# Projecting the first half of chunk 0 by blocks of the contraction, with twelve accumulation groups open in six PSUM banks

## The chip, the core and the metric

One core of one Trainium2 chip runs the kernel. The metric is the device time in microseconds (us) of one execution. PE is TensorE, PEld its weight loads, DVE VectorE, ACT ScalarE, POOL GpSimd and SP the engine that issues the DMAs. Times "at 7.13" are us from the start of the profiled span.

## The reference, cut to what matters

```python
x = A_x                                   # 1 x 2048 x 512, bf16
xn = layernorm(x)
s = A_ref(xn, wqkv, wo)                   # q, k, v = xn @ wqkv (512 x 1536); dilated local attention; @ wo
g = silu(B_ref(xn, w_gate, w_up, w_down)) # gelu(xn @ w_gate) * (xn @ w_up) @ w_down
return x + s * g
```

The contraction of `xn @ wqkv` runs over 512 rows, which are four blocks of 128.

## The kernel before

The kernel works on four chunks of 512 rows, each made of four tiles of 128. A tile must be normalized (VectorE), transposed (PE) and copied out of PSUM (ScalarE or VectorE) before PE can multiply it with `wqkv`. Chunk 0 is projected in halves: tiles 0 and 1 first, while tiles 2 and 3 arrive. `wqkv` is read in three column loads, q, then k, then v. While PE waits for data it multiplies constants ("warm-ups"), because its clock starts at half speed.

```python
for t in range(TPQ - 1):
    load_x(t)
load_w(wqkv_sb, A_wqkv, 0, D)                      # the columns of q
load_x(TPQ - 1)
for i in range(1, 3):
    load_w(wqkv_sb, A_wqkv, i * D, (i + 1) * D)    # of k, then of v
# ... cut ...
warm_up(18, TQ // 2)
warm_up(4, P)
first_moments(0)
first_moments(1)
first_normalize(0)
transpose(0)
first_normalize(1)
warm_up(4, P)                      # between the tiles' transposes
transpose(1, parts=2)              # two half copies, both on ScalarE
warm_up(4, P)
first_moments(2)
# ... cut: tile 3's moments, the normalizations of tiles 2 and 3 ...
for dks in ((0, 1), (2, 3)):       # q of the first half: 16 matmuls of 256 columns
    for fo in range(NC):
        project(qs[fo], wqkv_sb, fo * P, 0, 0, HQ, dks)
# ... cut: the copies of q, then k in halves, then v in one piece of 512 columns ...
def qkv(j, fo, i0=0, n=TQ, ps=None):
    # ... cut ...
        vst = sm4.tile([P, TQ], BF16, name="vst")
        nc.scalar.activation(out=vst[:], in_=ps, func=AF.Copy)
        nc.sync.dma_start(out=vT[c * P : (c + 1) * P, lo : lo + TQ], in_=vst[:])  # 4 stores of v per chunk
```

v goes to DRAM in four stores of 128 KB per chunk and comes back rearranged as `v_arr`, in four loads of 520 KB.

The softmax here doesn't subtract the row's maximum and nothing guards it: scores larger than these inputs give would overflow.

## Time and profile before

| | before |
|---|---|
| time, median of the first three runs | 229.21 us (229.19 to 229.28) |
| span of the profiled execution (229.35 us) | 227.65 us |
| clock of PE rises to full | at 6.75 |
| transposes of tile 0, of tile 1 start | 5.19, 6.02 |
| first projection matmul | 7.13 |
| transposes of tile 4 (the first after the projection of chunk 0) | 18.01 |
| last matmul starts | 223.94 |

The rows are starts read from the trace. Between 7.13 and 223.94 PE hardly ever waits, so an event moved at the start moves the end by the same amount, unless another wait takes it back.

In this execution the three columns of `wqkv` landed at 6.44, 8.11 and 10.26.

### The profile page before, as it was taken

How to read it: one execution, taken by the hardware profiler on the slowest of the kernel's cores; microseconds unless marked ns; L12 is line 12 of the kernel's file. 1: busy time of each engine (PE TensorE's matmuls, PEld its weight loads, DVE VectorE, ACT ScalarE, POOL GpSimd, SP SyncE). 2: the span in 40 equal slices, each digit the busy share in tenths (PEclk: the TensorE clock that was granted, in tenths of full speed). 3: DMA queues.
4: the chain of work that ended last, by engine and by line, in shares of the span. 5: the costliest groups of instructions: out<-in, count | busy, mean ns of one | idle time of the engine just before them, and what ended most of it. 6: DMA issues, size and time to landing. Idle time of an engine off the chain costs nothing.

```text
span 227.6 us, 3610 instructions
## 1 busy us (share of the span) xinstructions
PE 223.2 (98%) x1320; PEld 107.4 (47%) x1320; DVE 150.4 (66%) x274; ACT 135.0 (59%) x220; POOL 18.1 (8%) x67
## 2 busy tenths in 40 slices
PE   8999999999999999999999999999999999999993
PEld 6874444444444444444444444444444444444453
DVE  4693980899995578979904759924944358971434
ACT  3779779767532666767751566667753357656210
POOL 1047601000040000230000000000000000000000
PEclk9999999999999999999999999999999999999999
DMA  5999399972039911100219921110207950001001
GB/s 167 371 396 387 88 216 175 226 204 76 19 76 206 217 30 29 23 14 0 93 33 199 208 83 27 22 23 0 92 14 150 197 140 0 0 1 32 0 34 60
DMA packets 31266, 24.64 MB, mean 108 GB/s; under 512 B 10896, under 2 KB 31248, under 8 KB 31248
## 3 DMA queue, kind: packets, MB, share of 16 engines
q1 hardware_dynamic: 31248, 24.41, 44.4%
q8 instruction: 10, 0.16, 0.3%
q14 instruction: 8, 0.07, 0.2%
HBM read 18.74 MB, written 4.34 MB: 101 GB/s over the span
## 4 chain that ended last, share of the span: by engine, by line
PE 97%; ACT 1%; DVE 0%; issue 0%; DVEq 0%
PE y_ps L428 21%; PE u_ps L245 21%; PE g_ps L245 21%; PE qkv_ps L245 17%; PE s_ps L444 6%; PE L_ps L323 3%; PE o_ps L391 3%; PE warm_ps L227 2%; PE q_ps L245 1%; PE tr L210 1%; ACT L416 1%; PE den_ps L343 0%; ACT xnT L219 0%; ACT ge L416 0%; ACT vst L269 0%; DVE m L452 0%
## 5 line engine op out<-in xcount | busy, mean ns | idle before, releaser
L245 PE MATMUL u_ps<-xnT,wu_sb 128*128 128x512 bf16 x224 | 57.5, 379 | 0.0
L245 PE MATMUL g_ps<-xnT,wg_sb 128*128 128x512 bf16 x224 | 57.5, 379 | 0.0
L428 PE MATMUL y_ps<-wd_sb,h 128*128 128x512 bf16 (+1 forms) x238 | 49.9, 367 | 0.0
L420 DVE TENSOR_TENSOR h<-ge,u 128x512 bf16<-128x512 bf16 x56 | 23.8, 425 | 32.4 <-ACT u L418 30.9
L416 ACT ACTIVATE ge<-g_ps 128x512 bf16<-128x512 f32 x56 | 33.5, 598 | 16.4 <-PE g_ps L245 16.2
L418 ACT ACTIVATE u<-u_ps 128x512 bf16<-128x512 f32 x56 | 33.5, 598 | 16.1 <-PE u_ps L245 16.1
L305 DVE TENSOR_TENSOR pk<-q_sb,k_sb 128x1024 bf16<-128x1024 bf16 (+1 forms) x56 | 39.0, 761 | 4.6 <-ACT k_sb L266 4.6
L245 PE MATMUL qkv_ps<-xnT,wqkv_sb 128*128 128x512 bf16 (+1 forms) x208 | 40.6, 355 | 0.0
L377 DVE TENSOR_TENSOR pv<-E,v_arr 128x1024 bf16<-128x1024 bf16 (+1 forms) x48 | 39.7, 862 | 0.0
L428 PEld LDWEIGHTS <-h 128*128 128x128 bf16 x238 | 23.0, 98 | 25.9 <-issue 1.3
L245 PEld LDWEIGHTS <-wu_sb 128*128 128x128 bf16 x224 | 21.9, 98 | 26.7 <-issue 0.3
L245 PEld LDWEIGHTS <-wg_sb 128*128 128x128 bf16 x224 | 21.6, 98 | 26.4 <-issue 0.8
L245 PEld LDWEIGHTS <-wqkv_sb 128*128 128x128 bf16 x224 | 21.7, 98 | 19.7 <-DMA xnT<-xn 0.3
L436 ACT ACTIVATE sl<-y_ps 128x512 bf16<-128x512 f32 (+1 forms) x17 | 9.7, 572 | 32.6 <-PE y_ps L428 32.6
L452 DVE TENSOR_TENSOR m<-s_ps,sl 128x512 bf16<-128x512 f32 (+1 forms) x17 | 11.1, 655 | 18.4 <-PE s_ps L444 18.4
L403 DVE TENSOR_TENSOR oT<-o_ps,rb 128x1024 bf16<-128x1024 f32 x8 | 9.4, 1219 | 12.3 <-DMA rb<-rs_d 12.3
L444 PE MATMUL s_ps<-wo_sb,oT 128*128 128x512 bf16 (+1 forms) x68 | 14.8, 367 | 0.0
L195 POOL TENSOR_TENSOR rstd<-rstd,mhalf 128x1 f32<-128x1 f32 x12 | 7.9, 662 | 68.7 <-DVE rstd L192 68.7
L266 ACT ACTIVATE k_sb<-qkv_ps 128x512 bf16<-128x512 f32 (+1 forms) x20 | 10.2, 516 | 3.5 <-PE qkv_ps L245 3.2
L269 ACT ACTIVATE vst<-qkv_ps 128x512 bf16<-128x512 f32 x16 | 9.6, 597 | 4.5 <-PE qkv_ps L245 4.5
L263 ACT ACTIVATE q_sb<-qkv_ps 128x512 bf16<-128x512 f32 (+1 forms) x16 | 8.7, 544 | 3.2 <-PE qkv_ps L245 3.0
L444 PEld LDWEIGHTS <-oT 128*128 128x128 bf16 x68 | 6.6, 98 | 7.2
(49 smaller groups left out, 116.1 us busy)
## 6 DMA issues: line engine op xcount, KB each, us to landing
v_arr<-vT SPq DMA_DIRECT2D x16, 520.0 KB, 8.7
vT<-vst SPq DMA_DIRECT2D x16, 128.0 KB, 1.7
out_dram<-o_t SPq DMA_DIRECT2D x15, 128.0 KB, 3.2
wg_sb<-in_B_w_gate_dram SPq DMA_DIRECT2D x2, 896.0 KB, 9.8
wu_sb<-in_B_w_up_dram SPq DMA_DIRECT2D x2, 896.0 KB, 11.0
wd_sb<-in_B_w_down_dram SPq DMA_DIRECT2D x1, 1792.0 KB, 12.4
wqkv_sb<-in_A_wqkv_dram SPq DMA_DIRECT2D x3, 512.0 KB, 4.9
x_sb<-in_A_x_dram SPq DMA_DIRECT2D x3, 512.0 KB, 10.7
```

Of the source, the lines that this page charges most:

```text
L245: nc.tensor.matmul(ps, lhsT=w[:, dk, lo : lo + P], rhs=xnT[j][:, dk, i0 : i0 + n], start=(dk == 0), stop=(dk == NC - 1),)
L266: nc.scalar.activation(out=k_sb[j][:, c, lo : lo + n], in_=ps, func=AF.Copy)
L269: nc.scalar.activation(out=vst[:], in_=ps, func=AF.Copy)
L305: nc.vector.tensor_tensor(out=st[j]["pk"][w][:, c0 : c0 + n, :], in0=st[j]["q"][:, c0 : c0 + n, :], in1=k_sb[j][:, c0 : c0 + n, off : off ...
L377: nc.vector.tensor_tensor(out=pv[:, d : d + n, :], in0=st[j]["E"][:, wh, :].unsqueeze(1).to_broadcast([P, n, TQ]), in1=st[j]["va"][:, 4 * ...
L416: nc.scalar.activation(out=ge[:], in_=g_ps[:], func=AF.Gelu_apprx_tanh)
L418: nc.scalar.activation(out=u[:], in_=u_ps[:], func=AF.Copy)
L420: nc.vector.tensor_tensor(out=h[:], in0=ge[:], in1=u[:], op=ALU.mult)
L428: nc.tensor.matmul(y[:], lhsT=st[j][fc][:, tt * P : (tt + 1) * P], rhs=wd_sb[:, fc, cols], start=(fc == 0), stop=(fc == NF - 1),)
L436: nc.scalar.activation(out=sl[:], in_=y[:], func=AF.Silu)
L444: nc.tensor.matmul(s[:], lhsT=st[j]["oT"][:, g, tt * P : (tt + 1) * P], rhs=wo_sb[:, g, cols], start=(g == 0), stop=(g == NC - 1),)
L452: nc.vector.tensor_tensor(out=m[:], in0=s[:], in1=sl[:], op=ALU.mult)
```

## The change

The intent is to let the projection start with part of the weights. If the contraction is taken block by block, all of q, k and v of the first half can be worked on with the first 128 rows of `wqkv`. That needs twelve open sums (4 q, 4 k, 4 v, each 256 columns wide), two in each of six PSUM banks (PSUM is the memory that PE writes its results into; the kernel's two pools there hold four banks each). A product with a matrix of zeros opens each bank, in place of a warm-up. Besides that, VectorE's order at the start is changed, the first half copy of tile 1 goes to VectorE, the third set of warm-ups goes, the first half of v is copied out by VectorE, and v is stored in two pieces of 256 KB instead of four of 128 KB.

```diff
+    for i in range(2):
+        for t in (2 * i, 2 * i + 1):
+            load_x(t)
+        for k in (2 * i, 2 * i + 1):
+            nc.sync.dma_start(out=wqkv_sb[:, k, :], in_=A_wqkv[k * P : (k + 1) * P, :])
 # ... cut: in place of the three column loads ...
-            if copy is None:
+            if copy is None or k % 2:
 # ... cut: two stores of v per chunk ...
-    warm_up(18, TQ // 2)
+    warm_up(6, TQ // 2)
+    quad = att.tile([P, NC, 2, HQ], F32, name="qk_ps", tag="quad")
+    pairs = [(8 + 2 * i, mm.tile([P, 2, HQ], F32, name="v_ps", tag="mm")[:]) for i in range(2)]
+    pairs += [(2 * i, quad[:, i]) for i in range(4)]
+    for _, ps in pairs:
+        nc.tensor.matmul(
+            ps, lhsT=zero[:], rhs=nc.const_aps.tensor(1.0, [P, 2, HQ], BF16),
+            start=True, stop=False,
+        )
     warm_up(4, P)
+    first_stats(0)
     first_moments(0)
+    first_stats(1)
+    first_rstd(0)
     first_moments(1)
-    first_normalize(0)
+    normalize(0)
     transpose(0)
-    first_normalize(1)
+    first_rstd(1)
+    normalize(1)
     warm_up(4, P)
-    transpose(1, parts=2)
-    warm_up(4, P)
+    transpose(1, parts=2, copy=nc.vector.tensor_copy)
 # ... cut ...
+    for dk in range(NC):
+        for n, (fo, ps) in enumerate(pairs):
+            for i in range(2):
+                nc.tensor.matmul(
+                    ps[:, i, :],
+                    lhsT=wqkv_sb[:, dk, (fo + i) * P : (fo + i + 1) * P],
+                    rhs=xnT[0][:, dk, 0:HQ],
+                    start=False,
+                    stop=(dk == NC - 1 and i == 1),
+                )
+            if dk == 2 and n in (2, 5):
+                transpose(2 + (n == 5), copy=nc.vector.tensor_copy)
+    for fo, ps in pairs:
+        copy_out(0, fo, ps, 0, HQ, 2, nc.vector.tensor_copy if fo >= 8 else None)
 # ... cut: the second half, also two sums to a bank, v in halves ...
```

More of the change, by code (lines that the diff above doesn't have):

```diff
@@ L70 @@
     sm4 = pool("sm4", 4)
+    vsp = pool("vsp", 2)
     xnp = pool("xnp", 6)
@@ L95, in load_w @@
         )
-    for t in range(TPQ - 1):
-        load_x(t)
-    load_w(wqkv_sb, A_wqkv, 0, D)
-    load_x(TPQ - 1)
-    for i in range(1, 3):
-        load_w(wqkv_sb, A_wqkv, i * D, (i + 1) * D)
+    for i in range(2):
[3 more added lines that the diff above has]
+            nc.sync.dma_start(out=wqkv_sb[:, k, :], in_=A_wqkv[k * P : (k + 1) * P, :])
     load_x(TPQ, TPQ)
@@ L122 @@
     nc.vector.memset(zpad[:], 0.0)
+    zero = const.tile([P, P], BF16, name="zero")
+    nc.vector.memset(zero[:], 0.0)
     ident = const.tile([P, P], BF16, name="ident")
@@ L176, with first_stats @@
     nc.scalar.activation(out=std[:, 0, :], in_=epsc[:], func=AF.Sqrt, bias=epsc[:], scale=1.0)
+    def first_stats(t):
+        nc.vector.bn_stats(out=stats[:, t, :], in_=x_sb[:, t, :])
     def first_moments(t):
-        nc.vector.bn_stats(out=stats[:, t, :], in_=x_sb[:, t, :])
         nc.vector.bn_aggr(out=mv[:, t, :], in_=stats[:, t, :])
@@ L183, in first_moments, with first_rstd @@
         )
-    def first_normalize(t):
+    def first_rstd(t):
         nc.vector.reciprocal(out=rstd[:, t, :], in_=std[:, t, :])
-        normalize(t)
     def moments(t):
@@ L241, in transpose_by_dma, with project @@
             )
-    def project(ps, w, lo, j, i0=0, n=TQ, dks=range(NC)):
-        for dk in dks:
+    def project(ps, w, lo, j, i0=0, n=TQ):
+        for dk in range(NC):
             nc.tensor.matmul(
@@ L251, in project, with copy_out, qkv @@
             )
-    st = [dict(pk={}, pv={}) for _ in range(NJ)]
-    def qkv(j, fo, i0=0, n=TQ, ps=None):
+    st = [dict(pk={}, pv={}, vst={}) for _ in range(NJ)]
+    def copy_out(j, fo, ps, i0=0, n=TQ, m=1, copy=None):
         which, c = divmod(fo, NC)
-        if fo == 0 and i0 == 0:
-            st[j]["q"] = qp.tile([P, NC, TQ], BF16, name="q_sb")
-        if ps is None:
-            ps = mm.tile([P, n], F32, name="qkv_ps", tag="mm")[:]
-            project(ps, wqkv_sb, fo * P, j, i0, n)
         if which == 0:
-            nc.scalar.activation(out=st[j]["q"][:, c, i0 : i0 + n], in_=ps, func=AF.Copy)
+            if "q" not in st[j]:
+                st[j]["q"] = qp.tile([P, NC, TQ], BF16, name="q_sb")
+            dst = st[j]["q"][:, c : c + m, i0 : i0 + n]
         elif which == 1:
-            lo = PAD + i0
-            nc.scalar.activation(out=k_sb[j][:, c, lo : lo + n], in_=ps, func=AF.Copy)
-        else:
-            vst = sm4.tile([P, TQ], BF16, name="vst")
-            nc.scalar.activation(out=vst[:], in_=ps, func=AF.Copy)
-            lo = PAD + j * TQ
-            nc.sync.dma_start(out=vT[c * P : (c + 1) * P, lo : lo + TQ], in_=vst[:])
+            dst = k_sb[j][:, c : c + m, PAD + i0 : PAD + i0 + n]
+        else:
+            if c // 2 not in st[j]["vst"]:
+                st[j]["vst"][c // 2] = vsp.tile([P, 2, TQ], BF16, name="vst")
+            dst = st[j]["vst"][c // 2][:, c % 2 : c % 2 + m, i0 : i0 + n]
+        if copy is None:
+            nc.scalar.activation(out=dst, in_=ps, func=AF.Copy)
+        else:
+            copy(out=dst, in_=ps)
+        if which == 2 and (c + m) % 2 == 0 and i0 + n == TQ:
+            r, lo = slice((c // 2) * 2 * P, (c // 2 + 1) * 2 * P), PAD + j * TQ
+            nc.sync.dma_start(
+                out=vT[r, lo : lo + TQ].rearrange("(c p) n -> p c n", p=P),
+                in_=st[j]["vst"][c // 2][:],
+            )
+    def qkv(j, fo):
+        ps = mm.tile([P, 1, TQ], F32, name="qkv_ps", tag="mm")
+        project(ps[:, 0, :], wqkv_sb, fo * P, j)
+        copy_out(j, fo, ps[:])
     def load_v(j, wls=range(WL)):
@@ L504 @@
     at(("glu", NJ - 1, 12), sums, NJ - 1)
-    HT = TPQ // 2
-    HQ = HT * P
-    warm_up(18, TQ // 2)
+    HQ = TPQ // 2 * P
+    warm_up(6, TQ // 2)
[7 more added lines that the diff above has]
+        )
     warm_up(4, P)
+    first_stats(0)
     first_moments(0)
+    first_stats(1)
+    first_rstd(0)
     first_moments(1)
-    first_normalize(0)
+    normalize(0)
     transpose(0)
-    first_normalize(1)
+    first_rstd(1)
+    normalize(1)
     warm_up(4, P)
-    transpose(1, parts=2)
-    warm_up(4, P)
-    first_moments(2)
-    first_moments(3)
-    first_normalize(2)
-    first_normalize(3)
-    q4 = att.tile([P, NC, TQ], F32, name="q4_ps", tag="quad")
-    qs = [q4[:, fo, 0:HQ] for fo in range(NC)]
-    for dks in ((0, 1), (2, 3)):
-        for fo in range(NC):
-            project(qs[fo], wqkv_sb, fo * P, 0, 0, HQ, dks)
-    for fo in range(NC):
-        qkv(0, fo, 0, HQ, qs[fo])
-    transpose(HT, copy=nc.vector.tensor_copy)
-    for fo in range(NC, 2 * NC):
-        qkv(0, fo, 0, HQ)
-        if fo == NC:
-            transpose(HT + 1, copy=nc.vector.tensor_copy)
+    transpose(1, parts=2, copy=nc.vector.tensor_copy)
+    for t in (2, 3):
+        first_stats(t)
+        first_moments(t)
+    for t in (2, 3):
+        first_rstd(t)
+        normalize(t)
+    for dk in range(NC):
+        for n, (fo, ps) in enumerate(pairs):
[6 more added lines that the diff above has]
+                    stop=(dk == NC - 1 and i == 1),
+                )
+            if dk == 2 and n in (2, 5):
+                transpose(2 + (n == 5), copy=nc.vector.tensor_copy)
+    for fo, ps in pairs:
+        copy_out(0, fo, ps, 0, HQ, 2, nc.vector.tensor_copy if fo >= 8 else None)
     for t in range(TPQ, 2 * TPQ):
@@ L538 @@
     sum_constants()
-    for fo in range(2 * NC):
-        qkv(0, fo, HQ, HQ)
-    for i in range(NC):
-        run("qkv", 0, i)
-        run("qkv", 0, NC + i)
-        qkv(0, 2 * NC + i)
+    for n, fo in enumerate((0, 2, 4, 6, 8, 10)):
+        if n < TPQ:
+            run("qkv", 0, n)
+        ps = mm.tile([P, 2, HQ], F32, name="qkv_ps", tag="mm")
+        for i in range(2):
+            project(ps[:, i, :], wqkv_sb, (fo + i) * P, 0, HQ, HQ)
+        copy_out(0, fo, ps[:], HQ, HQ, 2)
     at(("glu", 0, 0), transpose_by_dma, TPQ + 2, (0, 1))
```

## The prediction

> **What bounds the kernel now.** I read the page first. TensorE (PE) is busy 98% of a 227.6 us span, and it is 97% of the chain that ended last, so only PE time counts.
>
> ```profile
> span 227.6 us, 3610 instructions
> PE 223.2 (98%) x1320; PEld 107.4 (47%) x1320; DVE 150.4 (66%) x274; ACT 135.0 (59%) x220; POOL 18.1 (8%) x67
> PE 97%; ACT 1%; DVE 0%; issue 0%; DVEq 0%
> ```
>
> The change touches the start (and the stores of v), so I then read the chain of waits for the first 40 us in order of time (start us, us, what):
>
> ```profile
> 0.84 4.43 PE warm_ps L227 x22
> 5.26 0.54 PE tr L210 x4
> 5.80 0.43 PE warm_ps L227 x4
> 6.23 0.44 PE tr L210 x4
> ...
> 6.69 0.39 ACT xnT L219
> 7.09 0.04 issue
> 7.13 1.91 PE q_ps L245 x16
> 9.04 0.22 PE tr L210 x4
> ...
> 9.92 8.27 PE qkv_ps L245 x60
> ```
>
> The projection starts at 7.13 us, after the last transpose of tile 1 and ScalarE's half copy of it, and then never stops. Before it everything on PE runs at half speed: four transposes take 0.44 us at 6.23 and 0.22 at 9.04. From 7.13 to the transposes of tile 4 at 18.01 PE has no gap: 64 matmuls of 256 columns, 16 of 512 and 8 transposes. The trace's starts are 0.109 us apart for 256 columns, 0.216 for 512 and 0.056 for a transpose, and 64 x 0.1091 + 16 x 0.2158 + 8 x 0.056 = 10.88 us, which is the whole stretch. So the weights are not late for the q-then-k-then-v order: there is no stall there to win.
>
> The timeline of VectorE and ScalarE shows what leads to 7.13 (start us, us, engine, line, operation; in brackets the idle time before it):
>
> ```profile
> 4.56 0.13 DVE L186 RECIPROCAL rstd<-std 128x1 f32<-128x1 f32 x1
> 4.68 0.29 ACT L181 ACTIVATE std<-mv,epsc 128x1 f32<-128x1 f32 x1 [0.44 <-DVE rstd L186]
> 4.73 0.41 DVE L201 TENSOR_SCALAR xn<-x_sb,mv,rstd 128x512 bf16<-128x512 bf16 x1
> ...
> 6.69 0.66 ACT L219 ACTIVATE xnT<-tr 128x256 bf16<-128x256 bf16 x2 [0.26 <-PE tr L210]
> 9.30 0.42 DVE L221 COPY xnT<-tr 128x512 bf16<-128x512 bf16 x1 [0.58 <-PE tr L210]
> 11.63 0.69 DVE L190 BATCH_NORM_STATS2 stats<-x_sb 128x6 f32<-128x512 bf16 x1 [1.25 <-DMA x_sb<-in_A_x_dram]
> ```
>
> Tile 0's normalization (4.73 to 5.14) releases the first transpose at 5.19. After that PE's own queue, with four warm-ups between the two tiles, sets the pace.
>
> **What the Trainium skill says.** "TensorE: Matmul & The Clock Gate", "Wait — 56ns, not 53.3ns?": a warm matmul costs N/2.4 ns plus about 2.5. The trace agrees (109.1 and 215.8 ns), so two matmuls of 256 cost 2.4 ns more than one of 512. Same page, "What's actually happening": the clock is at half until a busy, free-running window of about 3.4 us has passed. The trace agrees in kind: half pace until about 6.8 us, full at 7.13. "VectorE: DVE Perf Modes", "The TRN2 errata": a PSUM to SBUF op takes 120 + FD/Accel cycles at 0.96 GHz. For the 512-column bf16 copy at 2x that is 392 ns; the trace has 425, 33 more. "PSUM — Partial Sum Buffer", "PSUM bank collisions raise a hardware error": two engines must not access one bank at once. No run shows that, but the built program has it: ScalarE's half copy of tile 1 now waits for VectorE's half.
>
> **The change part by part.**
>
> 1. Warm-up. 18 x 256 + 4 x 128 columns = 5120 become 6 x 256 + 6 x 512 (the zero products that open the six banks) + 4 x 128 = 5120. Same columns, same half pace, so the last is issued at about 4.95 and the next may start at 5.06. Cost 0.
>
> 2. VectorE's order: the first reciprocal now precedes tile 1's aggregate. The reciprocal (0.13) moves from 4.56 to about 4.35, the aggregate stays at 4.46 to 4.64, and normalization 0 starts at about 4.56 and ends at 4.97 instead of 5.14. Transposes 0 then follow the warm-up without a gap, at 5.06; before, the start of the second transpose (5.277) implies 5.17. Gain 0.11. Normalization 1 ends at about 5.59, and transposes 1 are due at 5.06 + 8 x 0.1067 = 5.91, so it does not hold them. They end at about 6.54 instead of 6.66.
>
> 3. First half copy of tile 1 on VectorE. ScalarE took 384 ns. By the formula plus the 33 ns measured above, VectorE takes (120 + 128)/0.96 + 33 = 291 ns (an estimate). Gain 0.09. Against it: the first weight load now waits for that copy too in the built program, where before it ran ahead (6.77). Cost 0 to 0.10, as a weight load takes 0.10. The third set of four warm-ups goes; it was in no chain.
>
> 4. So the first projection matmul comes at about 6.58 + 0.29 + 0.06 = 6.93 to 7.03, against 7.13: 0.10 to 0.20 earlier.
>
> 5. The stretch itself: 96 matmuls of 256 columns + 8 transposes = 96 x 0.1091 + 0.45 = 10.92 us instead of 10.88, as v is now in halves. Cost 0.04. The tr4 transposes then start at about 17.9.
>
> 6. Weights. The three column loads landed at 6.44, 8.11 and 10.26 us. Reading the same 2.1 MB cumulatively, I estimate the row blocks at about 5.8, 6.8, 8.7 and 10.3; PE asks for them at 6.9, 8.3, 9.6 and 11.3. Tiles 2 and 3 of x come after two row blocks, at about 7.1 and 7.4 (3.9 and 6.8 before), are normalized by 9.4 and 9.9, and are transposed at about 10.2 and 11.1. Everything is hidden with 0.8 us or more to spare.
>
> 7. Copies. VectorE gets two 128x512 fp32 copies of v (0.69 us each, as its fp32 PSUM products of that size), at about 11.9 to 13.2. Moments of tiles 4 to 7 (1.0 us each) therefore start at 13.1 instead of 11.6, and normalization 4 ends at about 17.5 instead of 16.1, when PE wants it at 17.9: hidden by only 0.3 us. ScalarE has four copies of 0.60 from about 12.3 to 14.7 and then one per 0.87 us; no bank is wanted before it is free.
>
> 8. Afterwards. The last v copy, tile 4's copy, the Gelu table load and the first Gelu follow each other on ScalarE as before; the second u matmul still waits for that Gelu's bank (0.2 us at 21.26) and shifts with the rest. Two stores of 256 KB replace four of 128 KB per chunk; the loads of v stand behind the same bulk transfers, and nothing after 21.3 us in PE's record waits on them.
>
> Sum: 0.10 to 0.20 gained, 0.04 lost, so about 0.1 us off 229.21: 229.1.
>
> **Rivals.**
>
> (a) The clock. With the third warm-ups gone, PE is idle from about 6.5 to 6.95, just where the half pace ended before. If the window that counts no longer passes as busy, the next one ends about 3.4 us later. Matmuls from 6.95 to about 10.2 then run at half pace: +1.6 us, 230.7. For it: a window from about 0 to 3.4, in which PE worked from 0.84, did not lift the clock. Against it: the window before 6.8 would still be some 88% busy. I give it 1 in 10.
>
> (b) VectorE becomes the wait. If the v copies take 0.2 us longer each, or x tiles 4 to 7 land after 13.1 (11.6 before), tr4 waits for normalization 4: 0.1 to 0.5 us lost, 229.2 to 229.6. Speaking for it: only 0.3 us of slack. Against: all durations are measured ones.
>
> (c) The weights really are a gate and the row blocks remove it, giving 0.5 us or more, 228.6. The gapless stretch from 7.13 and the landing at 6.44 speak against it. The reverse, a row block landing late, has 0.8 us of slack.
>
> **Range and chances.** The working gives 229.0 to 229.2, with both ends of the weight-load term. The three runs differ by 0.09. I widen to 228.85 for a better start, and to 229.5 for rival (b); rival (a) lies outside. 2% is 4.6 us, more than any of these can move, so "within 2%" is almost certain.
>
> **What would show it.** Right: first projection matmul at 6.9 to 7.05; then no gap to tr4 at about 17.9; the four row blocks' landings before their first use; one gap of 0.2 us at about 21.15, none later. Wrong: 256-column matmuls 0.21 us apart after 7 us (a); a wait of tr4's weight load for VectorE's xn (b); a wait for a load of wqkv (c).

## More of the kernel before

VectorE multiplies `v_arr` in chunk 0's attention ("pv") and, behind that, q by k of chunk 1 ("pk").

The prediction shows the page's head, the chain of waits and the timeline of this start. One more part of the page of before is needed later, the DMA issues (size of one, median us from issue to landing):

```profile
v_arr<-vT SPq DMA_DIRECT2D x16, 520.0 KB, 8.7
vT<-vst SPq DMA_DIRECT2D x16, 128.0 KB, 1.7
```

These are medians; the trace also gives the landing of each one.

## The result, and the profile after

The kernel after takes 229.13 us (median of 6 runs, 228.84 to 229.63) against 229.21 for before in the same rounds (6 runs, 228.99 to 229.28). The ratio is 0.9999, with a 95% interval of 0.9986 to 1.0012: the same time. Ratios here are the mean time of one kernel's runs over that of the other's of the same rounds, so they are not quite the ratio of the medians that stand beside them.

The total is where it was predicted, but the way to it is not. The page of after, the row of busy times and the DMA issues:

```profile
PE 222.3 (98%) x1326; PEld 107.1 (47%) x1326; DVE 151.8 (67%) x278; ACT 132.2 (58%) x209; POOL 25.0 (11%) x67
...
vT<-vst SPq DMA_DIRECT2D x8, 256.0 KB, 2.2
```

PE still carries the span (227.37 us). The chain of waits of after, at the start (start us, us, what; "issue" is time in which the engine waited for nothing that the profile shows):

```profile
5.01 0.40 PE tr L214 x4
5.40 0.25 PE warm_ps L231 x4
5.65 0.04 issue
5.69 0.40 PE tr L214 x4
6.12 0.30 DVE xnT L225
6.42 0.14 issue
6.55 0.60 PE v_ps L554 x4
...
9.34 0.03 issue
9.37 0.61 PE v_ps L554 x4
```

The reader is to see two things. First, four warm-ups took 0.25 us at 5.40; in before they took 0.43 at 5.80. The clock was already at full speed here: its record rises at 4.29, and in before at 6.75. The projection therefore started at 6.55 instead of 7.13. Second, the chain breaks at 9.34: PE waits. The list of PE's weight-load waits after the projection's start (us in total, times, longest us) names the reason, and before had no such line:

```profile
PEld L554 <- DMA wqkv_sb<-in_A_wqkv_dram: 0.3, 1, 0.3
```

The third row block landed at 9.32. PE wanted it 24 matmuls after its start, at 6.55 + 24 x 0.109 = 9.17. From the starts in the trace, this cost 0.20 us. What remained of the lead at tile 4's transposes is 0.33 us (17.69 against 18.01), and it stays to the last matmul (223.62 against 223.94); the span is 0.28 us shorter, as is the time of the profiled executions (229.07 against 229.35).

So one trace says "0.3 us faster", while six runs say "the same". In the two traces the clock rose at different times after the start (this is called the clock's phase below), which no kernel here chose, and that was the first thing to test.

### The profile page after: what moved, and what is told of

Read it like the earlier page. It is cut to its first block, busy times and chain, and to the rows that moved or that the text cites. A ratio compares the mean times of both kernels' runs of the same rounds, so it can differ in the third digit from the quotient of the medians.

```text
span 227.4 us, 3595 instructions
## 1 busy us (share of the span) xinstructions
PE 222.3 (98%) x1326; PEld 107.1 (47%) x1326; DVE 151.8 (67%) x278; ACT 132.2 (58%) x209; POOL 25.0 (11%) x67
## 4 chain that ended last, share of the span: by engine, by line
PE 95%; DVE 1%; ACT 1%; DMA 1%; issue 0%; DVEq 0%
PE y_ps L443 21%; PE u_ps L249 21%; PE g_ps L249 21%; PE qkv_ps L249 16%; PE s_ps L459 6%; PE L_ps L338 3%; PE o_ps L406 3%; PE qk_ps L554 2%; DMA x_sb<-in_A_x_dram 1%; PE v_ps L554 1%; ACT L431 1%; DVE stats L182 1%; PE tr L214 1%; PE den_ps L358 0%; ACT ge L431 0%; ACT vst L273 0%
## 5 line engine op out<-in xcount | busy, mean ns | idle before, releaser
L249 PE MATMUL qkv_ps<-xnT,wqkv_sb 128*128 128x512 bf16 (+1 forms) x192 | 37.0, 352 | 0.0
L249 PEld LDWEIGHTS <-wqkv_sb 128*128 128x128 bf16 x192 | 18.8, 98 | 17.5
L273 ACT ACTIVATE vst<-qkv_ps 128x512 bf16<-128x512 f32 x14 | 8.4, 597 | 3.7 <-PE qkv_ps L249 3.7
L273 ACT ACTIVATE k_sb<-qkv_ps 128x512 bf16<-128x512 f32 x14 | 8.4, 601 | 3.2 <-PE qkv_ps L249 3.2
L273 ACT ACTIVATE q_sb<-qkv_ps 128x512 bf16<-128x512 f32 x14 | 8.3, 603 | 3.0 <-PE qkv_ps L249 3.0
```

Of the source, the lines that this page charges most:

```text
L249: nc.tensor.matmul(ps, lhsT=w[:, dk, lo : lo + P], rhs=xnT[j][:, dk, i0 : i0 + n], start=(dk == 0), stop=(dk == NC - 1),)
L273: nc.scalar.activation(out=dst, in_=ps, func=AF.Copy)
```

## The experiments

**Theory.** The rearranged start by itself saves some 0.1 to 0.2 us at one and the same clock phase, as step 4 of the prediction has it; the additional lead of the first trace is the clock's phase. **Rival 1.** The start saves nothing or costs time, because something in it has become slower that the early clock hid. **Rival 2.** Loads, not the clock, decide: the wait for the third row block is a fixed cost of the change. (The expectations for after_again, half_on_act and x3_later held this last view: each counts on that wait.)

Times below are medians, each batch of runs on one chip beside the kernel before. Before took 229.34 us (229.02 to 229.79, 11 runs) in the first batch (after_again, half_on_act, start_alone, x3_later), 229.48 (229.00 to 230.19, 11) in the second (late_open, no_mid_warm, rows_alone, open_alone) and 229.11 (228.78 to 229.63, 11) in the third (late_open_2, before_no_mid, early_table, all_three). All kernels gave correct results. What the traces show (start us; "lead" is how much earlier than in before tile 4's transposes start; negative is later):

| kernel | clock full at | transposes of tile 0 | of tile 1 | first projection matmul | third row block lands | lead at tile 4 |
|---|---|---|---|---|---|---|
| before | 6.75 | 5.19 | 6.02 | 7.13 | | 0 |
| after | 4.29 | 5.01 | 5.69 | 6.55 | 9.32 | 0.33 |
| after_again | 6.66 | 5.06 | 6.17 | 7.23 | 8.53 | -0.15 |
| half_on_act | 6.08 | 5.06 | 6.17 | 7.03 | 9.05 | 0.06 |
| start_alone | 6.67 | 5.06 | 5.91 | 7.02 | | -0.18 |
| x3_later | 4.13 | 4.91 | 5.59 | 6.46 | 8.13 | 0.01 |
| late_open | 4.19 | 5.00 | 5.68 | 6.55 | 9.04 | 0.54 |
| late_open_2 | 5.44 | 5.06 | 5.70 | 6.56 | 8.89 | 0.53 |
| no_mid_warm | 4.28 | 5.06 | 5.73 | 6.61 | 9.08 | 0.48 |
| all_three | 6.77 | 5.05 | 5.56 | 6.64 | 9.24 | 0.40 |
| rows_alone | 6.11 | 5.16 | 5.99 | 6.91 | 9.02 | -1.90 |

### after_again: the change once more

No edit.

> The changed kernel once more, unedited, for more executions and a second trace. My theory: the change has two parts that nearly cancel. An earlier start of the projection (VectorE order, half copy on VectorE) gains 0.1 to 0.3 us, and a new wait for the third row block of wqkv (0.20 us at 9.37 in its first trace) plus v in halves (0.04) gives most of it back. And a third thing is mixed in: the clock of PE rose at 4.29 us in the trace of after and at 6.75 in that of before, at a time that differs from execution to execution, so half of the 0.33 us between the two traces may be only that. Expected: 229.0 to 229.3, ratio to before 0.999 to 1.001, executions spread over 0.6 us or more, and another moment of the clock's rise in this trace, with the projection's start moved by it. Rival: the 0.33 us of the two traces are the change's own, and the median falls to 228.9 with more executions, ratio 0.9986.

Measured: 229.37 us (229.17 to 229.53, 5 runs), ratio 1.0002 (0.9991 to 1.0014). The ratio is as expected; the median is 0.07 us above the expected range, and the runs spread over 0.36 us, not over 0.6. The trace, of the slowest of the five (229.53 us), happens to have the clock rising at 6.66, nearly as in before, so it is the fair pair to it. Its chain of waits:

```profile
5.69 0.44 PE warm_ps L231 x4
6.13 0.04 issue
6.17 0.60 PE tr L214 x4
...
7.23 0.60 PE v_ps L554 x4
```

At the same phase the projection starts at 7.23, 0.10 us *later* than before's 7.13. Tile 1's transposes, due at 5.91, stand until 6.17, and what released them is PE's own last warm-up, which ended at 6.13. There was no wait for the third row block, which landed at 8.53, 0.79 us earlier than in the first trace, by the same program. So rival 2 falls: the wait is not a fixed cost. Rival 1 holds at this phase.

Where does PE's wait on itself come from? In the built program six of the eight banks are held open, so two are left for warm-ups and transposes. The four warm-ups between the tiles and tile 1's transposes get the same bank, and the transposes are made to wait until the warm-ups are through. In before they had different banks. The traces agree: in after, after_again and half_on_act alike the transposes start within 0.06 us after the end of the last warm-up (in after the normalization, done at 5.62, held them about as long, so the bank cost next to nothing there). start_alone and late_open_2 below show the two cases without the shared bank.

### start_alone: the start without the open groups

```diff
 # on the kernel before
-    first_normalize(1)
-    warm_up(4, P)
-    transpose(1, parts=2)
+    first_rstd(1)
+    normalize(1)
     warm_up(4, P)
+    transpose(1, parts=2, copy=nc.vector.tensor_copy)
 # with the order of VectorE of after, without the third warm-ups; tiles 2 and 3 transposed after the first and second k group
```

> Kernel before with the start of the changed one only (VectorE order, half copy on VectorE, no third set of warm-ups; tiles 2 and 3 transposed after the first and second k group), with the three column loads and q, then k, then v as before. My theory: the start is as early as in the changed kernel (6.55 us at the same clock), there is no later wait for weights, so 0.2 us below the changed kernel and 0.3 below before: 228.9, ratio 0.9985. Rival: the first row block (384 KB, landed 5.29) is what allows the early start, and here PE waits for the q columns (512 KB, landed 6.44 in the trace of before, perhaps 6.6): start at 6.6 to 6.8 and a total no better than the changed kernel's.

Measured: 229.39 us (228.93 to 230.07, 6 runs), ratio 1.0007 (0.9993 to 1.0021); 228.9 had been expected, so this missed. The trace, of the slowest of the six runs, has the clock at 6.67. Its timeline (idle time before it in brackets):

```profile
5.48 0.63 PE L228 MATMUL warm_ps<-const-bfloat16-1.0 128*128 128x128 bf16 x4
5.91 0.63 PE L211 MATMUL tr<-ident,xn 128*128 128x128 bf16 x4
```

With the same warm-ups, the same order of VectorE and the same phase, but free banks, tile 1's transposes start at 5.91 and the projection at 7.02. Against 6.17 and 7.23, the shared bank costs 6.17 - 5.91 = 0.26 us. 7.02 is inside step 4's 6.93 to 7.03: the start as predicted, once the overlooked wait is taken out; the theory's 0.1 us is there, and the bank eats it. Its lead of 0.11 was then lost: the columns of k landed at 8.97 (8.11 in before) and PE waited 0.26 us at 9.02, and 0.32 more at 100.04 for a DMA transpose (another 0.12 went near 39.9, for which the profile names no cause).

### half_on_act: ScalarE keeps both half copies

```diff
-    transpose(1, parts=2, copy=nc.vector.tensor_copy)
+    transpose(1, parts=2)
```

> Changed kernel with both half copies of tile 1's transposes back on ScalarE. The first projection matmul comes 0.09 us later (384 instead of 292 ns). My theory: PE then reaches the third row block 0.09 later and waits 0.09 less for it, so the transposes of tile 4 start at the same time and the total moves by less than 0.03 us. Rival (the start sets the end): the total is 0.09 us longer than the changed kernel's.

Measured: 229.78 us (229.44 to 230.29, 6 runs), ratio 1.0023 (1.0010 to 1.0036). ScalarE's half copies take 384 and 379 ns where VectorE's takes 292. The bank wait is there again (tile 1's transposes at 6.17). The clock had risen at 6.08, so these transposes ran at full pace (0.40 us, against 0.60 to their end in after_again), and the projection starts at 7.03. The executions are 0.4 us above those of after_again in the median. The start doesn't show that: its tile 4 is earlier than in before. In the trace it is lost at 153.59, where PE waits 0.46 us for a DMA transpose of chunk 3. Whether that wait comes with this edit or by chance was not settled; that all six runs are above after_again's median speaks for more than chance. Neither the theory (under 0.03 us) nor its rival (0.09 us) foresaw 0.4.

### late_open: one bank freed by opening the second v group later

```diff
-    pairs = [(8 + 2 * i, mm.tile([P, 2, HQ], F32, name="v_ps", tag="mm")[:]) for i in range(2)]
+    pairs = [v_pair(0)] + [(2 * i, quad[:, i]) for i in range(4)]
+    open_groups(pairs)
+    warm_up(2, TQ // 2)
 # ... cut ...
     transpose(1, parts=2, copy=nc.vector.tensor_copy)
+    pairs.insert(1, v_pair(1))
+    open_groups(pairs[1:2])
```

> Changed kernel with the second v group opened after tile 1's transposes instead of before the warm-up, two 256-column warm-ups in its old place. So tile 1's transposes no longer take the PSUM bank that the four warm-ups before them have just written. My theory: in the two traces of the changed kernel's order at a late clock rise (6.1 and 6.7 us), the transposes of tile 1 start at 6.17, 0.26 after their turn at 5.91, because they wait for that bank; here they start at 5.91 and the projection at 7.0 (late clock rise), so 0.1 to 0.25 us less in those executions and nothing with an early rise (the normalization of tile 1 gates them then); median 229.1 to 229.2, ratio to before 0.999. Rival: the wait is for the normalization or for VectorE in all cases, and the transposes stay at 6.17.

Measured: 229.15 us (228.79 to 229.34, 6 runs), ratio 0.9984 (0.9968 to 0.9999). Its trace fell on an early clock (4.19), where tile 1's normalization (done at 5.62) ends with the last warm-up (5.62), so it cannot show the bank's wait gone. The time is a little better than before's and just resolved.

### late_open_2: the same kernel, for another look

No edit to late_open.

> The kernel with the second v group opened late, unedited, for a second trace: the first had an early clock rise (4.2 us), where the normalization of tile 1 gates its transposes and the bank cannot be seen. My theory: if the clock rises after 6 us in this trace, tile 1's transposes start at 5.9 (not 6.17) and the projection at 7.0 (not 7.23). Rival: 6.17 and 7.23 as in the changed kernel. With an early rise again it tells nothing on this.

Measured: 228.88 us (one run, state unknown). The clock rose at 5.44, before the 6 us that the expectation asked for, so the starts of 5.9 and 7.0 could not be tested. The order of the starts and ends still shows what was asked:

```profile
5.47 0.39 PE L231 MATMUL warm_ps<-const-bfloat16-1.0 128*128 128x128 bf16 x4
5.70 0.39 PE L214 MATMUL tr<-ident,xn 128*128 128x128 bf16 x4
```

The warm-ups end at 5.86, and the transposes start at 5.70, 0.16 us before that end; with the shared bank they never started before it (ends of matmuls are modelled, but alike in all traces). So with another bank the wait is gone, in the changed kernel itself. The time of this one run proves nothing.

### no_mid_warm: the four warm-ups between the tiles taken away

```diff
     normalize(1)
-    warm_up(4, P)
     transpose(1, parts=2, copy=nc.vector.tensor_copy)
```

> Changed kernel without the four warm-ups between the transposes of tile 0 and tile 1. My theory: tile 1's transposes start when its normalization is done (5.6), the projection at 6.5 to 6.75 at any clock phase, so with a late rise 0.5 us earlier than the 7.23 of the changed kernel; then it waits 0 to 0.2 us for the third row block, which lands at 8.5 to 9.3 and is wanted 2.6 after the start. Total 0.2 to 0.4 below the changed kernel: 228.9, ratio 0.998. Rival (the clock): PE now idles some 0.5 us in the window that decides on the clock, and in some executions the clock rises one window (3.4 us) later: single executions 1 us or more above the others.

Measured: 228.96 us (228.86 to 229.19, 6 runs), ratio 0.9977 (0.9963 to 0.9991): faster than before by a resolved 0.2%. The chain of its start:

```profile
5.26 0.42 DVE xn L205
...
5.73 0.41 PE tr L214 x4
...
6.61 0.60 PE v_ps L553 x4
```

VectorE's normalization sets the transposes now, at 5.73, not PE's queue. At an early clock that gains nothing at the start (6.61 against 6.55). An earlier start could come at a late clock only, of which there is no trace of this kernel; all_three below, which has the same edit and one more at the start, shows it there.

### rows_alone and open_alone: each half of the change by itself

```diff
 # rows_alone, on the kernel before
-    for t in range(TPQ - 1):
-        load_x(t)
-    load_w(wqkv_sb, A_wqkv, 0, D)
-    load_x(TPQ - 1)
-    for i in range(1, 3):
-        load_w(wqkv_sb, A_wqkv, i * D, (i + 1) * D)
+    for i in range(2):
+        for t in (2 * i, 2 * i + 1):
+            load_x(t)
+        for k in (2 * i, 2 * i + 1):
+            nc.sync.dma_start(out=wqkv_sb[:, k, :], in_=A_wqkv[k * P : (k + 1) * P, :])
 # open_alone, on after: the reverse of these lines
```

> Kernel before with the four row-block loads of the changed one, and nothing else changed. My theory: q's third and fourth contraction blocks now wait for the row blocks that land at about 9 and 10.2 us, where q used to run from 7.1 to 8.9; PE stands still for about 2 us after the first eight matmuls and nothing gives it back: 231.2, ratio 1.009. Rival: with larger packets the row blocks land early enough, and it costs under 0.5 us.

> Changed kernel with the three column loads of before, and nothing else changed. My theory: the first matmuls are v's, whose columns land last, at about 10.3 us, so the projection starts at 10.3 instead of 6.6 to 7.2: 3 us more, 232.3, ratio 1.013. Rival: the clock stays up or the loads move and it costs under 1.5 us.

Measured: rows_alone 233.31 us (231.62 to 234.65, 3 runs), ratio 1.016 (1.0115 to 1.0205). The trace is of the quickest of the three; there q waits 1.29 us at 9.07 for the third block and 0.82 at 10.00 for the fourth. In the two others the mean granted clock is 0.993 and not 1.0, so they paid more. That is well over the 231.2 expected. open_alone took 234.57 us (234.53 to 234.64, 3 runs; 232.3 expected), ratio 1.022 (1.0201 to 1.0240). Its first matmul is one of v, and the columns of v land last, at 9.91. The windows of its start (its bounds, us, PE's busy time and instructions, then those of the other engines; the last three are granted clock, DMA share and GB/s):

```profile
4.74:8.15 3.41, 1.24 (x17) 0.84 (x15) 2.71 (x10) 1.61 (x5) 0.00 (x0) 1.00 1.06 351
8.15:11.57 3.42, 1.62 (x8) 1.19 (x9) 0.81 (x3) 0.16 (x1) 0.00 (x0) 0.50 1.07 387
11.57:14.98 3.41, 3.41 (x18) 2.41 (x17) 0.00 (x0) 0.00 (x0) 0.00 (x0) 0.50 1.05 405
```

The bounds 4.74, 8.15 and 14.98 are where this trace's record of the clock changes (up, down, up), and 11.57 halves the last stretch. After a window in which PE was busy for 1.24 of 3.41 us the clock dropped to half, the next with 1.62 did not lift it, and after the next, full one it rose. So from 9.95 to 14.98 the projection ran at half pace, which is about 2.5 us (half of that stretch) on top of the wait of 4.1 us for v's columns; after 14.98 the clock is full again. The wait had been expected, the clock's fall had not. A stretch at half pace is what rival (a) of the prediction feared, though here the clock fell again after it had risen, and by a longer idle time. So the two halves belong together: either alone costs 1.6 or 2.2%, both together nothing.

### x3_later: the third row block before tile 3

```diff
+    load_x(0); load_x(1); load_row_block(0); load_row_block(1)
+    load_x(2); load_row_block(2); load_x(3); load_row_block(3)
 # ... cut ...
-            if dk == 2 and n in (2, 5):
-                transpose(2 + (n == 5), copy=nc.vector.tensor_copy)
+            if dk >= 2 and n == 2:
+                transpose(dk, copy=nc.vector.tensor_copy)
```

> Changed kernel with the loads in the order x0, x1, w0, w1, x2, w2, x3, w3 and tile 3 transposed in the fourth block instead of the third. My theory: the third row block lands about 0.3 us earlier (near 9.0), PE's wait at 9.2 goes, and the total is 0.1 to 0.2 us below the changed kernel's, with a narrower spread. Rivals: the row block lands at the same time whatever is queued before it (then no change); or tile 3 now comes too late and PE waits for its normalization instead (0.2 us or more lost).

Measured: 229.60 us (229.24 to 231.34, 6 runs), ratio 1.0036 (1.0011 to 1.0060). The third block landed at 8.13 and its wait is gone. In exchange tile 3 landed at 8.53, its statistics stand before tile 2's normalization in VectorE's order, and that delay runs through VectorE to the normalization of tile 4. Its chain, at the end of the stretch:

```profile
17.62 0.33 DVE xn L211
...
18.00 0.40 PE tr L220 x4
```

PE lost 0.29 us at 10.02 and 0.31 at 18.00, both to VectorE. That is rival (b) of the prediction, in the size it was given there. In after the normalization of tile 4 ended at 17.30 and was wanted at 17.69, so it held there, with little to spare. The two waits do not account for the total: this trace is of the quickest of the six runs (229.24 us) and its last matmul starts 0.18 us before that of before. The two longest, 230.57 and 231.34, have no trace. They are 1 and 1.8 us above the others, which is the size of rival (a), a clock that rises later; nothing tests that.

### before_no_mid: the same warm-ups taken from the kernel before

The next question is whether no_mid_warm's edit needs the change at all.

```diff
     first_normalize(1)
-    warm_up(4, P)
     transpose(1, parts=2)
```

> Kernel before without the four warm-ups between the transposes of tile 0 and tile 1, the same removal that made the changed kernel 0.4 us faster. My theory: those warm-ups held tile 1's transposes in the kernel before too (6.02, with the normalization done at 5.66), so the start comes at 6.7 to 6.8 instead of 7.13 at a late clock rise; but the q columns land only at 6.4 to 6.7 and the k columns at 8.1 to 9.0 where they are wanted at 8.7, so it gains less than the row blocks allow: 0.2 to 0.3 us, ratio 0.999. Rival: it gains as much as the changed kernel did (ratio 0.9977), and the row blocks and open groups are worth nothing even then.

Measured: 229.64 us (228.96 to 230.02, 6 runs), ratio 1.0015 (0.9999 to 1.0031): nothing gained, where 0.2 to 0.3 us had been expected. The trace is of the slowest of the six runs (230.02 us). Yet its projection starts at 6.50 (clock full at 4.76), and it leads before by 0.63 us until 57.63. The lead vanishes at 61.3 to 61.9, where PE waits 0.98 us for chunk 1's products of q and k: at 61.9 it is 0.40 us behind before. It loses 0.28 more at 100.02 for a DMA transpose, as start_alone did. VectorE's timeline of this kernel says why:

```profile
42.00 1.22 DVE L377 TENSOR_TENSOR pv<-E,v_arr 128x2048 bf16<-128x2048 bf16 x1 [1.33 <-DMA v_arr<-vT]
...
52.09 9.72 DVE L305 TENSOR_TENSOR pk<-q_sb,k_sb 128x1024 bf16<-128x1024 bf16 x16
```

and the same rows of the kernel before:

```profile
41.26 1.23 DVE L377 TENSOR_TENSOR pv<-E,v_arr 128x2048 bf16<-128x2048 bf16 x1
...
51.70 9.72 DVE L305 TENSOR_TENSOR pk<-q_sb,k_sb 128x1024 bf16<-128x1024 bf16 x16
```

VectorE stood 1.33 us for the last load of `v_arr`, which landed at 41.92. Its work from the first pv to the last pk takes some 20 us with no gap above 0.17 us (41.26 to 61.41 in before), so the last product came at 61.81. PE, being 0.63 us ahead, wanted it at about 60.8. In before the last product ended at 61.41, just when PE came to it: the kernel before had no slack there, and as its load landed at 41.18, just before the first of these pv, an earlier start could only be returned unless the load came earlier too.

In after the load landed at 40.21. In the three kernels that keep the four stores of v and the column loads it landed at 41.18, 41.92 and 41.90 (before, before_no_mid, start_alone); in the nine profiled executions that have two larger stores and row blocks, after's first among them, between 40.06 and 40.80. So the earlier landing goes with the change, and before_no_mid shows, in one trace, what a start is worth without it. Which part of the change brings it was not settled: rows_alone, with four stores, had it at 40.05, and open_alone, with column loads, at 40.92, but both project so late that their stores are issued at other times too.

### early_table and all_three: more on top

```diff
 # early_table: no_mid_warm, and the table of Gelu loaded before the projection
     for t in (2, 3):
         first_rstd(t)
         normalize(t)
+    nc.scalar.preload_act_table(AF.Gelu_apprx_tanh)
 # all_three: early_table with late_open's edit
```

> Changed kernel without the warm-ups between tiles 0 and 1, and with the Gelu table loaded on ScalarE right after the last square root, in the 3 us that the open groups leave it idle (9.4 to 12.6 in the first trace of the changed kernel). My theory: the 1.28 us load leaves the chain last v copy, copy of tile 4, table load, first Gelu; the second u matmul group no longer waits 0.21 us; 0.2 us below the kernel without it: 228.75, ratio 0.9967 to 0.997. Rival: the load runs into the first q copies and PE waits for a bank instead, no gain; or a later Copy brings the old table back and it costs 1.3 us.

> As early_table, and with the second v group opened after tile 1's transposes, so that the product with zeros fills PE's idle time there. My theory: same start as without it (tile 1's bank is free in both, as the warm-ups between are gone), so within 0.1 us of early_table; what it may add is a clock that rises no later, so no single execution 1 us above the others. Rival: the product with zeros stands before the first projection at a late clock rise and delays it by 0.1 to 0.3 us.

Measured: early_table 228.73 us (228.67 to 229.72, 6 runs), ratio 0.9994 (0.9975 to 1.0013), where 0.9967 to 0.997 had been expected; all_three 229.18 us (228.77 to 230.16, 6 runs), ratio 1.0006 (0.9986 to 1.0026), and not within the 0.1 us of early_table that had been expected. In the traces both do what was meant: the wait of the second u product (0.21 us in before and after) is gone. Four of the six runs of early_table are at 228.67 to 228.74 and two at 229.43 and 229.72, so the interval doesn't separate it from before; what made those two longer has no trace. The chain of all_three is of use otherwise, since its clock rose late, at 6.77:

```profile
5.26 0.90 PE tr L214 x8
...
6.64 0.65 PE v_ps L563 x4
```

Without the warm-ups between them the eight transposes follow each other, and the projection starts at 6.64, at a clock phase at which after_again starts at 7.23 and before at 7.13. Without those warm-ups the start is nearly the same at both phases (6.61 early in no_mid_warm, 6.64 late in all_three), where after's moves between 6.55 and 7.23. It was tempting to explain no_mid_warm's narrow range of 0.33 us (0.79 for after) by that, but early_table and all_three, without the same warm-ups, range over 1.05 and 1.39 us.

no_mid_warm is the version that beats before by more than its interval, on its chip. The gain did not repeat: early_table and all_three contain its edit, on another chip, and neither is resolved from before. no_mid_warm and after ran in different batches, so that it beats after was not measured side by side.

### What the runs without a trace say of the phase

Every execution's mean granted clock is on record. In the trace of after it is 0.997, and the cause is that the clock falls 221.87 us after its rise, which for a rise at 4.29 comes before the span's end; in after_again, with a rise at 6.66, it is 1.0. A value below 1.0 therefore marks an early rise. (1.0 does not prove a late one: in x3_later the clock rose at 4.13 and did not fall within the span.) Of the first six runs of after five were below 1.0, of the five runs of after_again none. Sorted so, for after, for no_mid_warm (the one of its variants with three runs of each kind) and for before in the three batches:

| kernel, chip of | below 1.0, mean (runs) | at 1.0, mean (runs) |
|---|---|---|
| after, first comparison and first batch | 229.08 us (5) | 229.42 us (6) |
| no_mid_warm, second batch | 228.89 us (3) | 229.11 us (3) |
| before, first batch | 229.46 us (4) | 229.31 us (7) |
| before, second batch | (none) | 229.50 us (11) |
| before, third batch | 229.17 us (6) | 229.17 us (5) |

The 0.34 us of after is of the size that its two traces differ by (lead 0.33 against -0.15), though the groups come mostly from two chips. Before shows no gain from an early rise. That agrees with before_no_mid: before could not have used a lead. It is an argument from sorted runs and not an experiment, as no kernel here chose its phase. The other variants, with fewer runs below 1.0, do not agree among themselves: late_open has 228.96 us below (2 runs) and 229.17 at 1.0 (4), early_table 229.21 (2) and 228.89 (4), half_on_act 230.24 (1) and 229.76 (5).

## Why the prediction was right or wrong

The time (229.13 against 229.1 predicted) and the class were right, and the reason given for it holds: PE had no stall there for the new order to win, and everything at stake was some tenths of a us. That the sum also came out near its 0.1 us is luck: its gain at the start did not come as worked out, and an overlooked wait, an early clock and a late load took its place. By its steps:

1. Warm-up, cost 0: right. The transposes of tile 0 start at 5.06 at a late clock, as step 2 says.
2. VectorE's order, "transposes 1 are due at 5.06 + 8 x 0.1067 = 5.91, so it does not hold them": this step failed. The normalizations were in time (the first ended at 4.95 in after and 4.86 in after_again, predicted 4.97), but the transposes started at 6.17 in after_again. PE's wait for its own warm-ups in the shared bank, 0.26 us, was overlooked. The prediction had looked at the two half copies' bank and not at the warm-ups'.
3. Half copy on VectorE: right, 292 ns against 291. The exposed weight load is at the upper end of "0 to 0.10": from the copy's end to the first matmul after takes 0.146 us, before took 0.051, so 0.095.
4. Start at "6.93 to 7.03": wrong in both traces of after, in opposite directions. It is 7.23 at the late clock, which is step 2's 0.26 us (0.21 of it is left at the projection), and 6.55 when the clock rises at 4.29. start_alone, without the shared bank, gave 7.02. The step took the clock's rise as a fixed time, although it differs from one execution to the next: 4.13 to 6.77 in the profiles here. That the trace of before was a late one was chance.
5. The stretch of 10.92 us: right. In after_again it is 18.158 - 7.234 = 10.924.
6. Weights "hidden with 0.8 us or more to spare": wrong for the third block, estimated at 8.7. It landed between 8.53 and 9.32 in the executions with this order of loads, and when the start is early it is wanted at 9.17. In the first trace it cost 0.20 us: the prediction's own sign of being wrong, "a wait for a load of wqkv (c)", came. Tile 3 of x landed at 8.17 in after, predicted 7.4, which did no harm. Adding up bytes gives one number for a landing that moves by 0.8 us between two executions of the same program (8.53 and 9.32).
7. Copies: right. Normalization 4 ended at 17.30, wanted at 17.69; x3_later shows how soon that slack is used up.
8. Afterwards: right in what it says of PE, one gap of 0.21 us at 20.93 and none of size later in the trace. That "the loads of v stand behind the same bulk transfers" was too simple: the last landed 0.97 us earlier than in before (0.38 in after_again), and before_no_mid shows that a late one can take a lead away.

The rivals: (a), the clock one window late, was not seen: in the two traces of after it rose at 4.29 and 6.66, and none of its 11 executions took more than 229.63 us, where (a) was put at 230.7. (The mean granted clock cannot tell: it counts from the first rise, and before has 1.0 though it stood at half pace until 6.75.) In after_again PE was busy for 3.35 of the 3.41 us before the rise. (b) came in x3_later and not in after. (c) is right in its reverse form, a row block landing late.

The signs, put together: at a late clock the start is 0.10 us later, with 0.04 for the stretch, 0.15 in all; at an early one it is 0.58 earlier, less 0.20 for the third block and 0.04 for the stretch, about 0.33. Over all executions the difference is zero within 0.13%. The 0.58 is not all the change's own, as it sets an early clock against a late one: rows_alone has before's start, and with its clock rising at 6.11 it projects from 6.91 and not 7.13. half_on_act, at nearly the same phase (6.08), with the bank's wait and the slower half copy, starts at 7.03. What stays open: before's trace at an early clock, as its one profiled execution was a late one; why the same load lands up to 0.8 us apart; and which part of the change brings `v_arr` earlier.

## What to carry to other kernels

When one trace of each kernel is compared, look first at when PE's clock rose in each: here it moved by 2.6 us between executions, and with it one and the same changed kernel started the projection 0.10 us later or 0.58 us earlier than the one trace of before. Banks held open for accumulation are taken from the rotation of everything else, so list which instruction gets which bank and look for waits of an engine on itself. And a start made earlier is worth only what the slowest load downstream allows: find the next wait with no slack (here VectorE's products at 61 us) before expecting the gain to reach the end.

## What the Trainium skill lacked or had wrong

- "TensorE: Matmul & The Clock Gate", "What's actually happening": the page calls the window free-running and warns against fitting a model to one count of slow matmuls, which the prediction did all the same. It puts the variation at ±500 ns. Here the rise to full clock comes at 4.13 to 6.77 in fourteen profiled executions, a range of 2.64 us, and it moves the start of the projection (6.55 and 7.23 in one kernel). The page says that a busy window releases the clock, but not how busy: in open_alone a window with PE busy for 1.62 of 3.42 us (47%) did not and one with 3.41 of 3.41 did; nor did 2.52 of 3.36 us in all_three (75%), up to one window before the rise (6.77 - 3.41 = 3.36), while the window of the rise had 3.36 of 3.41. With the clock up, a window with 1.24 of 3.41 (36%) took it away, and one with 1.88 of 3.41 in rows_alone (55%, from 6.11) did not.
- "PSUM — Partial Sum Buffer" has collisions between engines, but nothing on the cost when PE's own instructions take turns in a bank because others are held open: 0.26 us here for one set of transposes behind four warm-ups.
- "ScalarE: Activation LUTs", "What ACT_TABLE_LOAD costs", gives about 1.28 us for a table load and about 1.38 more for a drain. The trace of after shows the load with 1.28 us at 18.99, right behind a copy that ended at 18.97, and the Gelu starting at 20.28, so no drain of that size before or after it.
- No page consulted says how far the landing of one and the same load moves from run to run: 8.53 and 9.32 us for the third row block in two executions of the same program.
